# A gated mix of linear attention and a feed-forward block on one core: the attention's middle part cut into smaller steps that one list orders, and its 64-row matmuls padded to 128 rows

## The chip, the core and the metric

The kernel runs on one NeuronCore of one Trainium2 chip. The engines are named as in the profile: PE is TensorE's matmul, PEld its weight load, DVE is VectorE, ACT is ScalarE, POOL is GpSimd, SP is SyncE (here it only issues DMAs). The metric is the device time of one execution in microseconds (us); of several executions the median counts.

## The reference

The input `x` has 2048 tokens of 576 features. Two blocks read it and a sigmoid gate mixes them. All data is float32.

```python
def _A_ref(x, wqkv, wo):                       # 32 heads of 18 features
    q, k, v = qkv[0], qkv[1], qkv[2]
    phi = lambda t: jnp.where(t > 0, t + 1, jnp.exp(t)) + 1e-6
    pq, pk = phi(q), phi(k)
    kv = jnp.einsum("bhsd,bhse->bhde", pk, v)
    z = jnp.einsum("bhsd->bhd", pk)
    num = jnp.einsum("bhqd,bhde->bhqe", pq, kv)
    den = jnp.einsum("bhqd,bhd->bhq", pq, z)[..., None] + 1e-6
    o = num / den
    return (lambda x, *d: x.transpose(*d))(o, 0, 2, 1, 3).reshape(B, S, D) @ wo
...
def _B_ref(x, w_gate, w_up, w_down):           # 4608 hidden features
    h = _gelu(g) * u
    return jnp.einsum("bsf,fd->bsd", h, w_down)
...
g = _sigmoid((x * gate_w).sum(-1, keepdims=True))
return g * a + (1 - g) * b
```

## The kernel before

**Precision.** PE works on a rounded float32 form (`F32R`). So each operand is split into a high part (ACT copies it, which rounds) and a low part (DVE or POOL subtracts the high part from the raw value), and a product is three matmuls: high by high, high by low, low by high. Hence most tiles have two halves.

**Stages.** First come the keys, their sums and the Gram matrices (until about 118 us of the span). Then the attention states are built (to about 146 us). The stage that the change touches comes next, from the masked states to the end of the mixing. Then gate and up projections run as chains of seven products each (a Strassen-like scheme over 2x2 blocks, steps `s1` to `s7`), and last the down projection.

**The stage of the change, step by step.** Tokens go in four blocks of 512 (`b`, in the order 2, 3, 0, 1), features in five groups (`g`), the first four of 128 rows and the last of 64.
- `query(b, g)`: PE multiplies queries into one of three PSUM buffers of the pool `banks` (14 matmuls of 512 columns, 10 in group 4). ACT takes Relu and Exp of it, DVE combines them into `r`. Only then is the buffer free. In group 4 a copy (ACT) and an addition (DVE) come first.
- `wo_load(g)` and `head_out(g)`: the output weight `wo` is loaded and split, PE multiplies it with the states into a buffer of the pool `pair` (two buffers), and ACT and DVE split the result into `KW[g]`. `rows_out` then copies two rows of `KW[4]` into each of the other four by DMA, and `rows_again` repeats the 64 rows of `KW[4]` in its upper half (high part only).
- `halves_of(b, g)` splits `r` into `hl` (two buffers), and `den(b, g)` adds it into the denominators on PE: one or two matmuls of 512 columns.
- `reciprocal(b, h)` inverts the denominators of half a block on DVE and stores them by DMA to DRAM; `reciprocals_load(b, h)` reads them back, spread over the partitions, as `rb`.
- `scale` multiplies `r` by `rb` on DVE, and `scaled_parts` splits the product into `p` (two buffers) on ACT and DVE, for a quarter `t` of a block.
- `mixed(b, t)`: 28 matmuls of 288 columns multiply `p` with `KW` into a `pair` buffer; ACT scales the result by the gate and a DMA stores it. In group 4 the product with the low part of `KW[4]` has only 64 rows (`QR[4]`): two of the 28 matmuls.

Between these stand pieces for later stages: sums of `x` blocks (`ahead_load`, `ahead_sums`, `ahead_store`), sums of up weights (`up_load`, `up_sums`, `up_store`), token sums (`token_load`, `token_sums`), and loads of the first gate and up weights.

**What sets the order.** The kernel is written under a manual schedule: each engine takes its instructions, and each DMA queue its transfers, in the order in which the Python code issues them, and waits at the first one whose operands are not there. In the stage of the change the order is the order of the calls, written out by hand. A pool gives out the buffer whose last reader stands earliest in that order.

Of the kernel before, what the change touches and what calls it, by code (L numbers as in the profile page):

```python
# [30 lines left out]


# [7 lines left out]
def tile_gated_mix(ctx, tc, xt, xs, xn, wk, wv, wq, wo, wgu, wdn, cst, out):  # L40
# [398 lines left out]
    def query(b, g):  # L439
        R = QR[g]  # L440
        if g == 0:
            r_of[b] = (r3p if b == 0 else rp).tile([128, NG, BS], F32, name="r")
            nc.vector.memset(r_of[b][:, NG - 1], 0.0)
        ps = bank()
        r = r_of[b][:R, g]
        ops = []
        for i in range(2):
            x, w = x_slot(b, i), qw[i]
            for kt in range(2):
                hi, lo = Q_HI[kt] + QO[g], Q_LO[kt] + QO[g]  # L450
                ops += [(w[:, hi:hi + 128], x[:, kt]), (w[:, hi:hi + R], x[:, 3 + kt])]
                if g < 4:
                    ops.append((w[:, lo:lo + 128], x[:, kt]))
            ops.append((w[:96, Q_HI[2] + QO[g]:Q_HI[2] + QO[g] + R], x[:96, 2]))
        for k, (wa, xa) in enumerate(ops):
            nc.tensor.matmul(ps[:wa.shape[1]], wa, xa, start=(k == 0), stop=(k == len(ops) - 1), skip_group_check=g == 4)  # L456
        if g == 4:
            nc.scalar.activation(r, ps[64:], AF.Copy)
            nc.vector.tensor_tensor(ps[:R], ps[:R], r, OP.add)
        nc.scalar.activation(r, ps[:R], AF.Relu, scale=-1.0)  # L460
        nc.scalar.activation(r, r, AF.Exp, scale=-1.0)
        nc.vector.scalar_tensor_tensor(r, ps[:R], 0.0, r, op0=OP.max, op1=OP.add)
# [82 lines left out]
    wo_t = {}  # L545

    def wo_load(g):
        raw = w_raw()[:, :D]
        nc.sync.dma_start(raw, wo[g])
# [5 lines left out]
    def states_out():  # L555
# [14 lines left out]
    def key_sums():  # L570
        for g in range(NG):
            R = QR[g]
            sg, z = sel[:R, g * 64:(g + 1) * 64], zc[:R, g:g + 1]
            for rows in (slice(0, R),) if g < 4 else (slice(0, 64), slice(64, 128)):
                nc.vector.tensor_scalar(zmk[rows, g, :64], sg, z, None, op0=OP.mult)
                nc.vector.scalar_tensor_tensor(zmk[rows, g, 64:], sg, z, f32(zmk[:R, g, :64]),
                                               op0=OP.mult, op1=OP.subtract)

    def head_out(g):
        R = VR[g]  # L580
        v = wo_t.pop(g)
        y = pair()
        kh, kl = kvt[:R, 0, g, :R], kvt[:R, 1, g, :R]
        for k, (ka, wl) in enumerate(((kh, 0), (kh, 1), (kl, 0))):
            for n in range(2):
                nc.tensor.matmul(y[:R, n, :288], ka, v[:R, wl, n * 288:(n + 1) * 288],
                                 start=(k == 0), stop=(k == 2))
        w = KW[g].rearrange("p h (n c) -> p h n c", n=2)
        split(w[:R, 0], w[:R, 1], y[:R, :, :288])

    def rows_out():
        for g in range(4):
            nc.sync.dma_start(f32(KW[g][126:]), f32(KW[4][64 + 2 * g:66 + 2 * g]))

    def rows_again():
        nc.scalar.activation(KW[4][64:, 0], f32(KW[4][:64, 0]), AF.Copy)

    hl_of, den_of, rb_of, p_of = {}, {}, {}, {}
    BT = BS // 128

    def halves_of(b, g):
# [8 lines left out]
    def den(b, g):  # L610
# [7 lines left out]

    WO = (4, 0, 1, 2, 3)
    wo_load(WO[0])  # L620
    wo_load(WO[1])
    states_out()
    key_sums()
    query(2, 4)
    halves_of(2, 0)
    halves_of(2, 1)
    query(3, 0)
    for g in range(NG):
        if g + 1 < NG:
            query(3, g + 1)  # L630
        head_out(WO[g])
        if g == 1:
            rows_out()
        if g + 2 < NG:
            wo_load(WO[g + 2])
            if g == 0:
                ahead_store(1)
                ahead_load(3)
                ahead_sums(2)
            elif g == 1:  # L640
                ahead_load(4)
            else:
                ahead_store(2)
                ahead_sums(3)
        elif g + 2 == NG:
            nc.sync.dma_start(xop_d[:, A11], f32(x_slot(2, 0)))
        den(2, g)
        if g + 2 < NG:
            halves_of(2, g + 2)
    ahead_load(5)  # L650
    ahead_sums(4)
    turn.close()
    weights.close()
# [23 lines left out]
    r3p = mixing.pool("r3p")  # L677
    qp = mixing.pool("qp", bufs=2)
    chunks = Scope()
    xcp = chunks.pool("xcp", bufs=2)  # L680

    HB = BS // 2

    def reciprocal(b, h):
        c = slice(h * HB, (h + 1) * HB)
        rb = rb_of[b, h] = qp.tile([128, NG, HB], F32, name="rb", bufs=3)
# [6 lines left out]
    def reciprocals_load(b, h):  # L693
# [6 lines left out]
    def reciprocals(b):  # L700
        for h in range(2):
            reciprocal(b, h)
        for h in range(2):
            reciprocals_load(b, h)

    def scale(b, t):
# [4 lines left out]
    def scaled_parts(b, t):  # L711
        r = r_of[b][:, :, t * 128:(t + 1) * 128]
        p = p_of[b, t] = qp.tile([128, 2, NG, 128], F32R, name="p")
# [4 lines left out]
    def scaled(b, t):  # L718
        scale(b, t)
        scaled_parts(b, t)  # L720

    def mixed(b, t):
        p = p_of.pop((b, t))
        y = pair()
        n = 0
        for g in range(NG):
            for a, wl, R in ((0, 0, 128), (0, 1, QR[g]), (1, 0, 128))[:3 if g < 4 else 2]:
                for i in range(2):
                    nc.tensor.matmul(y[:, i, :288], p[:R, a, g], KW[g][:R, wl, i * 288:(i + 1) * 288],  # L729
                                     start=(n == 0), stop=(n == 13))  # L730
                n += 1
        st = b * BT + t
        o = qp.tile([128, D], F32, name="ga")
# [4 lines left out]
    chunk = {0: Chunk(xcp, 0, 0)}  # L738

    def token_load(kt):  # L740
        chunk[kt] = Chunk(xcp, 0, kt)

    def token_sums(kt, part):
        if part == 0:
            chunk[kt].sums()
        else:
            chunk.pop(kt).summed(nc.gpsimd)

    halves_of(3, 0)
    reciprocals(2)  # L750
    ahead_store(3)
    ahead_store(4)
    ahead_sums(5)
    halves_of(3, 1)
    rows_again()
    nc.sync.dma_start(xop_d[:, A12], f32(x_slot(2, 1)))
    query(0, 0)
    query(0, 1)
    ahead_store(5)
    up_load(0)  # L760
    nc.sync.dma_start(xop_d[:, A22], f32(x_slot(3, 1)))
    den(3, 0)
    halves_of(3, 2)
    den(3, 1)
    halves_of(3, 3)
    query(0, 2)
    up_sums(0)
    up_load(1)
    token_load(1)
    den(3, 2)  # L770
    halves_of(3, 4)
    den(3, 3)
    scaled(2, 0)
    query(0, 3)
    up_sums(1)
    up_load(2)
    den(3, 4)
    scaled(2, 1)
    mixed(2, 0)
    reciprocals(3)  # L780
    query(0, 4)
    up_sums(2)
    up_store(0)
    up_store(1)
    scaled(2, 2)
    token_sums(0, 0)
    mixed(2, 1)
    halves_of(0, 0)
    halves_of(0, 1)
    scaled(2, 3)  # L790
    token_sums(0, 1)
    query(1, 0)
    up_store(2)
    mixed(2, 2)
    den(0, 0)
    halves_of(0, 2)
    query(1, 1)
    scaled(3, 0)
    den(0, 1)
    halves_of(0, 3)  # L800
    mixed(2, 3)
    token_load(2)
    scaled(3, 1)
    token_sums(1, 0)
    query(1, 2)
    den(0, 2)
    halves_of(0, 4)
    den(0, 3)
    mixed(3, 0)
# [438 lines left out]
```

## Time and profile before

| | |
|---|---|
| median of 3 runs | 1516.74 us (1513.53 to 1517.01) |
| the profiled execution | 1514.94 us, span 1513.1 us |
| PE busy | 1500.1 us, 99% of the span |
| DVE, ACT, POOL busy | 1013.6, 549.2 and 717.9 us |
| keys and Gram matrices | to 118 us of the span |
| states | 118 to 146 us |
| the stage of the change | 146 to 293.5 us |
| gate and up chains | 293.5 to about 1112 us |
| down projection | to the end |

The stage of the change ends, on PE, with the last matmul of `mixed(1, 3)`. The first four products of the first gate chain (`first_steps`) stand inside it. A matmul's row in the profile covers its whole way through the array, so rows of successive matmuls overlap: a matmul of 288 columns has a row of some 300 ns, though the next one starts much sooner. How fast PE really goes is read from the distance of starts. Idle time behind a row in square brackets counts only what lies between two such rows.

### The profile page before, as it was taken

How to read it: one execution, taken by the hardware profiler on the slowest of the kernel's cores; microseconds unless marked ns; L12 is line 12 of the kernel's file. 1: busy time of each engine (PE TensorE's matmuls, PEld its weight loads, DVE VectorE, ACT ScalarE, POOL GpSimd, SP SyncE). 2: the span in 40 equal slices, each digit the busy share in tenths (PEclk: the TensorE clock that was granted, in tenths of full speed). 3: DMA queues.
4: the chain of work that ended last, by engine and by line, in shares of the span. 5: the costliest groups of instructions: out<-in, count | busy, mean ns of one | idle time of the engine just before them, and what ended most of it. 6: DMA issues, size and time to landing. Idle time of an engine off the chain costs nothing.

```text
span 1513.1 us, 21566 instructions
## 1 busy us (share of the span) xinstructions
PE 1500.1 (99%) x8312; PEld 1318.2 (87%) x8312; DVE 1013.6 (67%) x1350; ACT 549.2 (36%) x716; POOL 717.9 (47%) x516
## 2 busy tenths in 40 slices
PE   9999999999999999999999999999999999999999
PEld 9999777878888888888888888888899999999999
DVE  8887677485665556665556665556678767777775
ACT  7554545333222332222332222332244344444431
POOL 2663531265645545545545545444257264644620
PEclk9999999999999999999999999999999999999999
DMA  7562473673332223332223322224777656565564
GB/s 248 173 195 87 156 277 141 224 278 109 139 118 91 105 104 139 140 116 93 104 105 139 139 109 101 104 105 166 281 259 276 214 168 214 167 214 179 203 201 134
DMA packets 98751, 246.53 MB, mean 163 GB/s; under 512 B 9104, under 2 KB 36432, under 8 KB 96216
## 3 DMA queue, kind: packets, MB, share of 16 engines
q1 hardware_dynamic: 95768, 235.58, 44.9%
q10 hardware_dynamic: 2880, 9.57, 1.8%
q8 instruction: 65, 1.06, 0.3%
q14 instruction: 38, 0.31, 0.1%
HBM read 156.80 MB, written 88.28 MB: 162 GB/s over the span
## 4 chain that ended last, share of the span: by engine, by line
PE 89%; DVE 3%; DMA 2%; ACT 2%; issue 1%; POOL 1%; SPq 1%; ACTq 0%; DVEq 0%; POOLq 0%
PE bank L878 53%; PE bank L1141 24%; PE pair L729 2%; PE pair L257 2%; PE pair L212 2%; PE kpair L212 2%; PE kpair L257 2%; PE bank L456 1%; DMA xsum_d<-xu 1%; DMA stage<-wdn 0%; DMA xo<-h_d 0%; DVE hl L607 0%; DMA xu<-wgu 0%; POOL wd L1027 0%; DMA raw<-wo 0%
## 5 line engine op out<-in xcount | busy, mean ns | idle before, releaser
L878 PE MATMUL bank<-xo,wg 128*128 128x512 f32 x1764 | 414.4, 395 | 0.6 <-DVE e L910 0.6
L878 PE MATMUL bank<-xo,wu 128*128 128x512 f32 (+1 forms) x1715 | 401.7, 395 | 0.0
L878 PEld LDWEIGHTS bank<-xo,wg 128*128 128x128 f32 x1764 | 332.1, 188 | 79.0 <-DVE e L910 1.0
L878 PEld LDWEIGHTS bank<-xo,wu 128*128 128x128 f32 (+1 forms) x1715 | 323.3, 189 | 75.3
L1149 DVE SCALAR_TENSOR_TENSOR acc<-bank,gate,acc 128x288 f32<-128x288 f32 x288 | 140.0, 512 | 68.7 <-PE bank L1141 65.9
L296 POOL TENSOR_TENSOR stage<-stage 128x384 f32<-128x384 f32 x132 | 153.7, 1184 | 52.2 <-DMA stage<-wgu 49.6
L919 ACT ACTIVATE p<-bank 128x512 f32<-128x512 f32 x72 | 43.0, 597 | 334.4 <-PE bank L878 334.4
L892 POOL TENSOR_TENSOR wg<-stage,wg 128x768 fp32r<-128x768 f32 (+1 forms) x34 | 72.9, 2145 | 178.4 <-ACT wg L891 177.1
L892 POOL TENSOR_TENSOR wu<-stage,wu 128x768 fp32r<-128x768 f32 (+1 forms) x34 | 79.6, 2342 | 147.8 <-ACT wu L891 146.5
L1141 PE MATMUL bank<-wd,xo 128*128 128x288 f32 x1008 | 135.8, 294 | 0.0
L1141 PEld LDWEIGHTS bank<-wd,xo 128*128 128x128 f32 x1008 | 134.1, 188 | 0.0
L1027 POOL TENSOR_TENSOR xo<-stage,xo 128x432 fp32r<-128x432 f32 x44 | 66.3, 1529 | 114.9 <-ACT xo L1025 111.2
L924 DVE TENSOR_TENSOR u<-bank,p 128x512 f32<-128x512 f32 x72 | 49.5, 687 | 94.7 <-PE bank L878 92.3
L1141 PE MATMUL bank<-xo 128*128 128x288 f32 x792 | 107.1, 295 | 0.1
L1141 PEld LDWEIGHTS bank<-xo 128*128 128x128 f32 x792 | 105.7, 188 | 0.5 <-DVE u L913 0.4
L1027 POOL TENSOR_TENSOR wd<-stage,wd 128x432 fp32r<-128x432 f32 x40 | 59.1, 1504 | 89.0 <-ACT wd L1025 89.0
L910 DVE TENSOR_TENSOR e<-bank,u 128x512 f32<-128x512 f32 x54 | 37.2, 691 | 77.3 <-PE bank L878 77.2
L910 DVE TENSOR_TENSOR f<-bank,u 128x512 f32<-128x512 f32 x54 | 37.2, 691 | 72.6 <-PE bank L878 72.3
L900 ACT ACTIVATE f<-f 128x512 f32<-128x512 f32 x54 | 34.1, 632 | 133.5 <-DVE f L910 133.5
L1032 POOL TENSOR_TENSOR stage<-stage 128x432 f32<-128x432 f32 x48 | 75.9, 1607 | 0.0
L938 DVE TENSOR_TENSOR u<-bank,u 128x512 f32<-128x512 f32 x72 | 49.8, 692 | 35.4 <-PE bank L878 33.2
L729 PE MATMUL pair<-kw,p 128*128 128x288 f32 x448 | 67.8, 306 | 1.4 <-ACT p L714 1.4
(197 smaller groups left out, 2324.2 us busy)
## 6 DMA issues: line engine op xcount, KB each, us to landing
h_d<-sx SPq DMA_DIRECT2D x108, 256.0 KB
stage<-wgu SPq DMA_DIRECT2D x34, 768.0 KB
xo<-h_d SPq DMA_DIRECT2D x29, 768.0 KB
e<-h_d SPq DMA_DIRECT2D x28, 768.0 KB
hraw<-h_d SPq DMA_DIRECT2D x27, 768.0 KB
h_d<-e SPq DMA_DIRECT2D x72, 256.0 KB
h_d<-f SPq DMA_DIRECT2D x72, 256.0 KB
stage<-wdn SPq DMA_DIRECT2D x6, 1728.0 KB
```

Source lines behind the costliest of these rows:

```text
L212: nc.tensor.matmul(out_t[:, :n], xa, kvw[i][:rows, r, lo:lo + n], start=(k == 0), stop=(k == 13))
L257: nc.tensor.matmul(y[:, n, :KH], a, p[:, n * KH:(n + 1) * KH], start=(k == 0), stop=(k == len(ops) - 1))
L296: nc.gpsimd.tensor_tensor(o, a, b, OP.subtract)
L729: nc.tensor.matmul(y[:, i, :288], p[:R, a, g], KW[g][:R, wl, i * 288:(i + 1) * 288], start=(n == 0), stop=(n == 13))
L878: nc.tensor.matmul(ps, w_, x_, start=start and i == 0, stop=i == 6, skip_group_check=not start)
L892: nc.gpsimd.tensor_tensor(w[:, i, 3:5], src[:, :, 0:2], f32(w[:, i, 0:2]), OP.subtract)
L910: nc.vector.tensor_tensor(es[i], a, b, OP.add)
L938: nc.vector.tensor_tensor(u3, c, u2, OP.add)
L1027: nc.gpsimd.tensor_tensor(w[:, 1, c], src[:, c], f32(w[:, 0, c]), OP.subtract)
L1032: nc.gpsimd.tensor_tensor(draw[:, o, c], draw[:, x, c], draw[:, y, c], OP.subtract)
L1141: nc.tensor.matmul(y, h[:, hl, g, t * 128:(t + 1) * 128], w[:, wl, g * 288:(g + 1) * 288], start=k in (1, 5) and n == 0, stop=n == len(ops ...
L1149: nc.vector.scalar_tensor_tensor(o, y, gate[:, 1, st:st + 1], o, op0=OP.mult, op1=OP.add)
```

## The change

The steps are cut smaller: `query` into `q` (PE), `qs` (the extra step of group 4), `qe` (ACT) and `qd` (DVE), with `qz` for the memory that has to be zero; `wo_load` into `wl` (load) and `ws` (split); `head_out` into `ho` (PE) and `he` (split); `mixed` into `m` (PE) and `mo` (ACT and store). `scale` and `scaled_parts` become `sc` and `sp`, `halves_of` becomes `h`, `den` becomes `n`, `reciprocal` and `reciprocals_load` become `rc` and `rl`; `ks` is one group of the key sums. One list of words, `PLAN`, says in which order all of them are issued, together with `al`, `as`, `ao`, `ul`, `us`, `uo` (the pieces for later stages), `tl`, `ts`, `tp` (token sums), `ro` and `rd` (the row copies), `xo`, `w`, `g`, `f` (first chain) and `o` (opening and closing of pools). The work itself is the same, with two exceptions: the two 64-row matmuls of `mixed` take all 128 rows, for which the upper half of the low part of `KW[4]` is set to zero once, and `r` is set to zero only where it must be.

```diff
+PLAN = """
+h20 wl4 q24 so q31 al3 h21 ws4 wl0 wl3 qs2 qe24 qz3 ks0 ks2 qe31 wl1 ao1 q30 qd24 ks3 ho4 qd31 ks1 n20 q32 ws0
...
+rl21 q01 qe00 tl0 q02 n30 qe02 qd02 n31 ao3 qd00 h32 qe01 ao5 q03 n32 sc21 ul0 xo2 h33 ul1 sc20 qd01 us0 h34 q04
+qe03 ul2 n33 sp20 n34 rd h00 sp21 rc30 us1 qs0 m20 sc22 m21 rc31 qd03 qe04 sp22 sc23 q11 us2 ts0 q10 tl1 rl30
...
+"""
...
-    def query(b, g):
+    def q(b, g):
...
+    def qe(b, g):
+        ps, r = q_of[b, g][:QR[g]], r_of[b][:QR[g], g]
+        nc.scalar.activation(r, ps, AF.Relu, scale=-1.0)
+        nc.scalar.activation(r, r, AF.Exp, scale=-1.0)
+
+    def qd(b, g):
+        ps, r = q_of.pop((b, g))[:QR[g]], r_of[b][:QR[g], g]
+        nc.vector.scalar_tensor_tensor(r, ps, 0.0, r, op0=OP.max, op1=OP.add)
...
-    def rows_again():
+    def ro(g):
+        nc.sync.dma_start(f32(KW[g][126:]), f32(KW[4][64 + 2 * g:66 + 2 * g]))
+
+    def rd():
         nc.scalar.activation(KW[4][64:, 0], f32(KW[4][:64, 0]), AF.Copy)
+        nc.vector.memset(f32(KW[4][64:, 1]), 0.0)
...
-            for a, wl, R in ((0, 0, 128), (0, 1, QR[g]), (1, 0, 128))[:3 if g < 4 else 2]:
+            for a, wl in ((0, 0), (0, 1), (1, 0))[:3 if g < 4 else 2]:
                 for i in range(2):
-                    nc.tensor.matmul(y[:, i, :288], p[:R, a, g], KW[g][:R, wl, i * 288:(i + 1) * 288],
+                    nc.tensor.matmul(y[:, i, :288], p[:, a, g], KW[g][:, wl, i * 288:(i + 1) * 288],
...
+    for word in PLAN.split():
+        name = word.rstrip("0123456789")
+        steps[name](*map(int, word[len(name):]))
```

The order changes on every engine. Three places show how.

First, the DMA queue of SP from the load of the constants (`cs`) to the copies of two rows into `kw` (`rows_out`). `raw<-wo` are the loads of the output weights, `xu<-xs` and `xsum_d<-xu` loads and stores of the sums for later. Before:

```order
L539 DMA cs<-cst 128x446
L549 DMA raw<-wo 128x576 x3
L315 DMA xsum_d_74<-xu 128x1024
L309 DMA xu<-xs 128x4x256
L593 DMA kw_1883<-kw_1887 2x1152
L593 DMA kw_1884<-kw_1887 2x1152
L593 DMA kw_1885<-kw_1887 2x1152
L593 DMA kw_1886<-kw_1887 2x1152
L549 DMA raw<-wo 128x576
L309 DMA xu<-xs 128x4x256
L549 DMA raw<-wo 128x576
```

The same queue after the change:

```order
L573 DMA cs<-cst 128x446
L583 DMA raw<-wo 128x576
L322 DMA xu<-xs 128x4x256
L583 DMA raw<-wo 128x576 x3
L328 DMA xsum_d_74<-xu 128x1024
L322 DMA xu<-xs 128x4x256
L583 DMA raw<-wo 128x576
L328 DMA xsum_d_75<-xu 128x1024
L631 DMA kw_1884<-kw_1887 2x1152
```

All five loads of `wo` now stand ahead of the row copies; before, two of them stood behind.

Second, DVE around the first two quarters of block 2 that are scaled and split (`r<-r,rb` is `scale`, `p<-r,p` the two subtractions of `scaled_parts`, `r<-bank,r` the last step of a query, `hl<-r,hl` that of `halves_of`). Before:

```order
L709 SCALAR_TENSOR_TENSOR r<-r,rb 128x5x128
L715 TENSOR_TENSOR p<-r,p 128x512
L716 TENSOR_TENSOR p<-r,p 64x128
L462 SCALAR_TENSOR_TENSOR r<-bank,r 128x512
L709 SCALAR_TENSOR_TENSOR r<-r,rb 128x5x128
L715 TENSOR_TENSOR p<-r,p 128x512
L716 TENSOR_TENSOR p<-r,p 64x128
L689 TENSOR_TENSOR rb<-rb,den 40x256
```

After, between the last step of a query and the reciprocals of block 3:

```order
L646 SCALAR_TENSOR_TENSOR hl<-r,hl 128x512
L701 SCALAR_TENSOR_TENSOR r<-r,rb 128x5x128
L646 SCALAR_TENSOR_TENSOR hl<-r,hl 128x512
L701 SCALAR_TENSOR_TENSOR r<-r,rb 128x5x128
L485 SCALAR_TENSOR_TENSOR r<-bank,r 128x512
L646 SCALAR_TENSOR_TENSOR hl<-r,hl 64x512
L707 TENSOR_TENSOR p<-r,p 128x512
L708 TENSOR_TENSOR p<-r,p 64x128
L635 MEMSET kw_1887 64x576
L646 SCALAR_TENSOR_TENSOR hl<-r,hl 128x512
L707 TENSOR_TENSOR p<-r,p 128x512
L708 TENSOR_TENSOR p<-r,p 64x128
```

The scaling and the subtractions of one quarter no longer follow each other on DVE; three other instructions or more stand between them, and the zeroing of `KW[4]` is among them.

Third, PE at the first three queries of block 0 and the denominators of block 3 (the numbers tell the PSUM buffers apart). Before:

```order
L456 MATMUL bank_2194<-xo_116,qw0_121 128x512 x7
L456 MATMUL bank_2194<-xo_116,qw1_122 128x512 x7
L456 MATMUL bank_2212<-xo_116,qw0_121 128x512 x7
L456 MATMUL bank_2212<-xo_116,qw1_122 128x512 x7
L616 MATMUL den_2234<-hl_2164,zmk_1888 128x512 x2
L616 MATMUL den_2234<-hl_2187,zmk_1888 128x512 x2
L456 MATMUL bank_2245<-xo_116,qw0_121 128x512 x7
L456 MATMUL bank_2245<-xo_116,qw1_122 128x512 x7
L616 MATMUL den_2234<-hl_2237,zmk_1888 128x512 x2
```

After:

```order
L467 MATMUL bank_2188<-xo_116,qw0_121 128x512 x7
L467 MATMUL bank_2188<-xo_116,qw1_122 128x512 x7
L467 MATMUL bank_2205<-xo_116,qw0_121 128x512 x7
L467 MATMUL bank_2205<-xo_116,qw1_122 128x512 x7
L467 MATMUL bank_2224<-xo_116,qw0_121 128x512 x7
L467 MATMUL bank_2224<-xo_116,qw1_122 128x512 x7
L655 MATMUL den_2239<-hl_2166,zmk_1888 128x512 x2
L655 MATMUL den_2239<-hl_2173,zmk_1888 128x512 x2
L467 MATMUL bank_2255<-xo_116,qw0_121 128x512 x7
L467 MATMUL bank_2255<-xo_116,qw1_122 128x512 x7
L655 MATMUL den_2239<-hl_2249,zmk_1888 128x512 x2
```

Three queries now stand in a row ahead of the denominators, and only two pairs of denominator matmuls stand between the third query and the fourth, for which one of the three buffers has to be free again.

More of the change, by code (lines that the diff above doesn't have):

```diff
@@ L437, in wv_make @@
         nc.gpsimd.tensor_tensor(w[:, 1], raw, f32(w[:, 0]), OP.subtract)
-    def query(b, g):
+    q_of = {}
+    def q(b, g):
         R = QR[g]
[L441 to L445, printed above, removed]
+        ps = q_of[b, g] = bank()
         ops = []
@@ L617, in den @@
                              stop=g == NG - 1, skip_group_check=True)
[L619 to L653, printed above, removed]
     class Chunk:
@@ L698, in reciprocals_load, with sc @@
                 ap=[[NG * HB, heads], [0, times], [1, NG * HB]]))
[L700 to L706, printed above, removed]
+    def sc(b, t):
         r = r_of[b][:, :, t * 128:(t + 1) * 128]
@@ L759, in tile_gated_mix @@
[L759 to L785, printed above, removed]
@@ L861, in tile_gated_mix, with w_, f_ @@
+    def w_(i):
+        (nc.sync if i else nc.scalar).dma_start(f32(W[i]), wp_d[i])
+    def f_(i):
+        first_steps[i]()
     GATE, UP = 0, 1
```

228 lines of the change are left out of this document (88 added, 140 removed).

## Prediction

> **What bounds the kernel now.** I read the page first, then the windows of the stage that the change touches, then the chain of work and the PE timeline inside it.
>
> ```profile
> PE 1500.1 (99%) x8312; PEld 1318.2 (87%) x8312; DVE 1013.6 (67%) x1350; ACT 549.2 (36%) x716; POOL 717.9 (47%) x516
> PE 89%; DVE 3%; DMA 2%; ACT 2%; issue 1%; POOL 1%; SPq 1%; ACTq 0%; DVEq 0%; POOLq 0%
> ...
> core 0: us, PE busy (x) PEld busy (x) DVE busy (x) ACT busy (x) POOL busy (x), PEclk, DMA share, GB/s
> 145.90:160.00 14.10, 13.04 (x60) 9.98 (x59) 10.62 (x32) 7.72 (x16) 2.81 (x2) 1.00 0.00 1
> 160.00:186.00 26.00, 23.54 (x104) 18.55 (x103) 18.35 (x23) 15.56 (x28) 19.70 (x19) 0.93 0.53 186
> 186.00:205.00 19.00, 18.82 (x102) 15.49 (x101) 11.77 (x16) 7.73 (x14) 2.40 (x4) 1.00 0.87 339
> 205.00:232.00 27.00, 25.65 (x138) 21.02 (x137) 20.77 (x29) 13.70 (x21) 12.68 (x14) 1.00 0.59 203
> 232.00:258.00 26.00, 23.57 (x133) 19.74 (x132) 16.93 (x26) 14.55 (x23) 5.08 (x4) 0.93 0.42 149
> 258.00:293.50 35.50, 35.50 (x226) 31.69 (x225) 18.53 (x26) 13.18 (x18) 7.03 (x4) 1.00 0.64 235
> 321.00:1112.00 791.00, 790.87 (x3413) 641.71 (x3412) 487.07 (x631) 215.62 (x285) 397.80 (x274) 1.00 0.36 130
> ```
>
> PE bounds nearly everything: 89% of the chain, and 790.87 of 791 us in the gate and up chains. What shortens PE's way through the stage of the change (145.9 to 293.5, 147.6 us) therefore shortens the whole, and nothing else there counts. DVE is busy in some 97 of these 147.6 us (the six rows), ACT and POOL less: none of them has too much to do; what they can do is be late.
>
> How much of the 147.6 us is work is read from the chain, where successive matmuls are merged without overlap.
>
> ```profile
> 118.88 3.23 PE bank L456 x14
> ...
> 277.14 16.41 PE pair L729 x112
> ...
> 1146.04 363.74 PE bank L1141 x2745
> ```
>
> A matmul of 512 columns takes 3.23 / 14 = 0.231 us, one of 288 columns 363.74 / 2745 = 0.1325. The stage holds, by the code, 208 wide ones in the queries (twelve of 14, four of 10), 36 in the denominators, 28 in the first gate chain, and 448 of 288 columns in `mixed` and 30 in `head_out`: 272 x 0.231 + 478 x 0.1325 = 62.8 + 63.3 = 126.1 us. So 147.6 - 126.1 = 21.5 us are lost, and they are of three kinds.
>
> *The 64-row matmuls.* The second row of the last fence is four `mixed` without a wait: 16.41 us where 112 x 0.1325 = 14.84 would do, 0.39 us too much in each. The weight loads show where:
>
> ```profile
> 284.81 0.29 PEld L729 LDWEIGHTS pair<-kw,p 64*128 64x128 f32 x2 [0.16 <-issue]
> 285.27 3.49 PEld L729 LDWEIGHTS pair<-kw,p 128*128 128x128 f32 x26 [0.17 <-issue]
> ...
> L729 PE MATMUL pair<-kw,p 64*128 64x288 f32 x32 | 8.4, 344 | 0.0
> ```
>
> The loader stands still for 0.16 us before the two 64-row loads and for 0.17 us after them, waiting for nothing that the profile shows. All 32 of them in 16 `mixed`: 16 x 0.39 = 6.3 us.
>
> *A halved clock.* In two windows the granted clock is 0.93 instead of 1.00. In the PE timeline these are the places:
>
> ```profile
> 169.67 0.63 PE L616 MATMUL den<-hl,zmk 128*128 128x512 f32 x2
> 171.78 0.53 PE L586 MATMUL pair<-wos,kvt 126*126 126x288 f32 x2 [1.48 <-ACT wos L551]
> 173.25 0.79 PE L586 MATMUL pair<-wos,kvt 126*126 126x288 f32 x4 [0.95 <-POOL wos L552]
> ...
> 174.23 8.09 PE L456 MATMUL bank<-xo,qw 128*128 128x512 f32 x28
> ...
> 198.04 4.08 PE L729 MATMUL pair<-kw,p 128*128 128x288 f32 x28
> ...
> 250.03 1.10 PE L616 MATMUL den<-hl,zmk 128*128 128x512 f32 x3 [0.22 <-DVE hl L607]
> 252.13 5.74 PE L729 MATMUL pair<-kw,p 128*128 128x288 f32 x28 [1.01 <-ACT p L714]
> ```
>
> Two queries take 8.09 us, where 2 x 3.23 + 0.16 for the last row's overlap = 6.6 would do, and one `mixed` 5.74 where another takes 4.08: 1.5 + 1.7 = 3.2 us. Both follow a few us in which PE waited again and again.
>
> *Waits.* The rest, 21.5 - 6.3 - 3.2 = 12.0 us: in part the idle times in brackets, in part the slow restart behind each, which rows that overlap hide.
>
> **Part 1: the padding.** It removes 0.39 us from each `mixed`, 6.3 us in all, for every row of 128-row matmuls in a stream goes at 0.1325. It adds one DVE write of 64x576 in `rd`; the nearest row of a DVE instruction of that size is the 0.7 us subtraction in the next fence. Only the last four matmuls of the first `mixed` need it, 24 x 0.1325 = 3.2 us after that starts; so it costs nothing, or at most 0.7 us without that cover. The bounds of the part are 6.3 and 0. A loss is excluded, since the padded loads are of the same shape as the 26 beside them. The rows of the loader decide, and I take 6.3. The Trainium skill speaks against it: "TensorE: Matmul & The Clock Gate", section "LDWEIGHTS (loading the stationary operand)", says that a load's time goes by its columns and that few rows take as long as 128, by which padding would bring nothing and the sum would be 6.3 us smaller; that the loads themselves take as long is so here, but the rows show the loss beside them.
>
> **Part 2: the waits that go.**
>
> ```profile
> 135.44 2.73 SPq L549 DMA_DIRECT2D raw<-wo  x3
> 160.67 2.70 SPq L593 DMA_DIRECT2D kw<-kw  x4
> 164.58 0.61 SPq L549 DMA_DIRECT2D raw<-wo  x1
> 171.04 0.68 ACT L551 ACTIVATE wos<-raw 128x576 fp32r<-128x576 f32 x1 [1.83 <-DMA raw<-wo]
> ...
> L715 DVE TENSOR_TENSOR p<-r,p 128x512 fp32r<-128x512 f32 x16 | 11.3, 705 | 15.3 <-ACT p L714 15.3
> L607 DVE SCALAR_TENSOR_TENSOR hl<-r,hl 128x512 fp32r<-128x512 f32 x16 | 13.5, 870 | 7.7 <-ACT hl L606 7.6
> L709 DVE SCALAR_TENSOR_TENSOR r<-r,rb 128x640 f32<-128x640 f32 x16 | 13.7, 859 | 0.3 <-DMA rb<-rden_d 0.2
> L690 DVE RECIPROCAL rb<-rb 40x256 f32<-40x256 f32 x8 | 14.0, 1745 | 0.3
> L689 DVE TENSOR_TENSOR rb<-rb,den 40x256 f32<-40x256 f32 x8 | 3.1, 388 | 1.7 <-ACT rb L688 1.6
> L301 DVE TENSOR_TENSOR xc<-xc 128x512 f32<-128x512 f32 x3 | 2.2, 739 | 0.1
> L460 ACT ACTIVATE r<-bank 128x512 f32<-128x512 f32 x13 | 7.6, 586 | 7.5 <-PE bank L456 7.5
> L461 ACT ACTIVATE r<-r 128x512 f32<-128x512 f32 x13 | 8.2, 633 | 0.4
> L462 DVE SCALAR_TENSOR_TENSOR r<-bank,r 128x512 f32<-128x512 f32 x13 | 8.7, 676 | 9.4 <-ACT r L461 9.3
> ```
>
> The hole at 170 to 174 is a queue matter: SP cannot issue the row copies before 160.67, since they wait for `KW[4]`, so the last load of `wo` goes out at 164.58, and its split waits until 171.04. In the new order all five loads stand ahead of the copies, where the first three went out at 135.44; the fifth now waits for a store and its buffer, by my walk still some 15 us ahead of its use. This hole and the halved clock behind it go. The others come from DVE: it waits 15.3 us in 16 pieces of nearly 1 us for ACT's half of a split, with denominators' `hl` queued behind. With `sc` apart from `sp` that time is filled with other work.
>
> **Part 3: the waits that come.** I walked the list with these durations. PE's path meets four places:
> - `q03` takes the buffer of `q02`, the first to be free in the list. From the end of `q02`, 0.59 + 0.63 + 0.68 = 1.9 us pass on ACT and DVE, and `qd00`, `h32` are queued behind on DVE; PE has only four denominator matmuls, 0.9 us, meanwhile. With the handoffs 1.2 us.
> - From the end of `n04` DVE owes two reciprocals (2 x 2.13), `h10`, `sc33`, `h11` (0.87, 0.86, 0.87) and 0.7 of `sp32`, 7.6 us, before `m32` can go through; PE has `q14`, `m31`, `n10`, 10 x 0.231 + 3.7 + 0.46 = 6.5. Wait 1.1 us.
> - From `n14` DVE owes `rc10`, two scalings, the token sums of four times 0.74 and `sp02`, 2.13 + 1.72 + 2.96 + 0.7 = 7.5 us; PE has two `mixed` of 3.7. Nothing to 0.5 us, say 0.3.
> - `n01` needs `h01`, which stands on DVE behind the first token sums: some 0.4 us.
>
> Together 3.0 us. That is the lower bound of waiting; the upper is the 12.0 us of before. The walk knows no restart losses and no late DMA, so I take the middle, 7.5 us. No idle of 3 us is left in it, and the 1.06 us in the window from 145.90 left the clock at 1.00; so I count no halved clock.
>
> **The sum.** The stage takes 126.1 + 7.5 = 133.6 us instead of 147.6: 14.0 us less. Behind it everything moves along unchanged if the next weights come in time:
>
> ```profile
> 288.36 0.34 SPq L882 DMA_DIRECT2D stage<-wgu  x1
> 310.02 10.03 PE L878 MATMUL bank<-xo,wg 128*128 128x512 f32 x42
> ```
>
> They are fetched once the last split of `p` frees the memory, 21.7 us before their use. In the new list `m12`'s rest, `m13` and the same ten products follow that split, so the cover stays. The profiled execution of 1514.94 us becomes 1500.9; the median of before lies 1.8 us above it, so I predict 1516.74 - 14.0 = 1502.7 us.
>
> **Rivals.** A measurement of this kernel tells about 0.3%, 4.5 us, from no change.
> - *The new order waits as long as the old, and only the padding counts* (12%): for it speaks that three of the four waits above are DVE queues as before; against it that the 170 hole has one cause, which goes. 6.3 us less, 1510.4.
> - *The padding brings nothing* (4%): the loader stands still at this place whatever the rows, and only the order counts: 14.0 - 6.3 = 7.7 us less, 1509.0. Against it, no other place of the four `mixed` has such a hole. The Trainium skill's rule on loads, above, would have it so.
> - *Almost nothing* (4%): both fall short, within 4.5 us of 1516.74.
> - *Slower, by late reciprocals* (5%). DVE takes its scalings in order, and with `sc21` ahead of `h33`, `qd01` and `h34` a late `rb` now stops the steps that free PSUM buffers and feed the denominators.
>
> ```profile
> 178.65 1.75 DVE L690 RECIPROCAL rb<-rb 40x256 f32<-40x256 f32 x1
> 189.68 0.83 DVE L709 SCALAR_TENSOR_TENSOR r<-r,rb 128x640 f32<-128x640 f32 x1 [0.16 <-DMA rb<-rden_d]
> ```
>
> From the end of the reciprocal (180.4) to its use 9.2 us pass, the last 0.16 of them waiting. In my walk `sc21`, `sc10` and `sc12` come 9 to 10 us behind theirs: at each, what the DMA takes beyond some 10 us is lost one for one. To be slower by 4.5 us it must lose 18.5 us at these three, 6 us each, so 16 us for what took 9.2: 1521. The load of the up weights, issued right behind the last `rb`, speaks for it; the DMA share, 0.64 in the last window of the stage, against it.
>
> **Numbers.** The forecast of waits between 3.0 and about 10 us has 75%. From its lower end, 18.5 us less, 1498.2, and some 1 us for the runs' scatter comes the low end, 1497; the padding alone gives the high end, 1510.5. Faster by over 0.3%: 75 + 12 + 4 = 91%; same 4%; slower 5%.
>
> **What would show it.** Right: the `mixed` without waits at 3.7 us each and no 64-row load among them; no ACT wait for `raw<-wo`; the last matmul of the stage some 14 us before 293.5; PEclk 1.00 throughout; a PE wait ahead of `q03`. The forecast is wrong if the padded `mixed` still takes 4.0 us, if DVE waits for `rb` for microseconds, or if a window shows the halved clock again.

## The result and the profile after

The changed kernel takes 1507.29 us (median of 6 runs, 1506.52 to 1507.93) beside 1515.83 us of the kernel before (6 runs): ratio 0.9945, 95% interval 0.9932 to 0.9957, so 8.5 us less by the medians. Forecast were 14.0 us less, 1502.7 us in a range of 1497 to 1510.5.

The timeline of PE, kernel after (start, us, engine, line, names, shape, count, and in brackets the idle time ahead with what ended it):

```profile
169.88 9.85 PE L467 MATMUL bank<-xo,qw 128*128 128x512 f32 x42
...
181.80 3.55 PE L467 MATMUL bank<-xo,qw 128*128 128x512 f32 x14 [1.14 <-DVE r L485]
...
188.68 7.44 PE L717 MATMUL pair<-kw,p 128*128 128x288 f32 x56
...
203.49 0.50 PE L655 MATMUL den<-hl,zmk 128*128 128x512 f32 x1 [0.22 <-DVE hl L646]
...
229.95 0.50 PE L655 MATMUL den<-hl,zmk 128*128 128x512 f32 x1 [0.25 <-DVE hl L646]
...
231.64 3.46 PE L717 MATMUL pair<-kw,p 128*128 128x288 f32 x24 [0.66 <-DVE p L707]
...
243.90 0.80 PE L655 MATMUL den<-hl,zmk 128*128 128x512 f32 x1 [4.15 <-DVE hl L646]
244.49 13.83 PE L717 MATMUL pair<-kw,p 128*128 128x288 f32 x84
...
273.97 11.64 PE L717 MATMUL pair<-kw,p 128*128 128x288 f32 x84 [1.73 <-ACT p L706]
286.44 5.17 PE L790 MATMUL bank<-xo,wg 128*128 128x512 f32 x21 [0.83 <-ACT ga L724]
...
302.98 7.37 PE L790 MATMUL bank<-xo,wg 128*128 128x512 f32 x31
```

The third chain of products, which began at 310.02, begins at 302.98: 7.0 of the 7.4 us between the two profiled runs (1514.94 and 1507.52) arise ahead of it. The first rows are as forecast: no hole at 170 to 174, a wait at `q03`, two `mixed` without waits in 7.44 us, so 3.7 each, and small waits at `n01` and around `m32`. Three waits were not on the list: 4.15 us ahead of `n14` (the last denominator matmul of block 1), 1.73 ahead of `m11`, 0.83 ahead of the first product behind the stage. And the three `mixed` from 244.49 (`m00` to `m02`) take 13.83 us for 84 matmuls, where 84 x 0.1325 = 11.1 would do. The windows around them show why (columns as in the prediction's windows, the granted clock third from the end):

```profile
238.00:243.30 5.30, 1.75 (x12) 1.31 (x10) 1.87 (x5) 3.94 (x7) 0.00 (x0) 1.00 0.80 278
243.30:250.10 6.80, 6.20 (x25) 6.11 (x26) 6.38 (x9) 1.07 (x3) 0.00 (x0) 0.50 0.66 272
```

The halved clock is there again, for 6.8 us, behind the long idle. So the stage took 286.44 - 146.20 = 140.2 us instead of 147.6. Against the 126.1 us of work that is 14.1 us lost: 2.65 by the clock (13.83 against 11.18 for the same 84 matmuls in the run with a buffer more, below) and 11.5 in waits. Of these 11.5 the brackets above show 8.98 us; the rest, as in the prediction's 12.0, comes out of the difference alone, and no row shows it.

What held `n14` is told by the chain of waits of the kernel after, in the same place (start, us, what):

```profile
229.03 0.75 ACT ga L724
...
229.81 8.48 DMA ga_d<-ga
...
238.37 0.75 ACT ga L724
...
240.09 0.14 ACT L743
240.23 1.15 issue
...
241.50 0.73 ACT p L706
...
243.24 0.61 DVE hl L646
...
243.90 0.80 PE den L655
```

`mo31` writes `ga` at 229.03 and its store goes out at 229.81. `ga` has two buffers, so `mo32` needs the one that this store reads, and the store lands after 8.5 us. ScalarE takes its instructions in the list's order: behind `mo32` (238.37) stand the issue of the gate weights' load (`w0`), the gelu table load (`g`, L743, ending at 241.4), `sp00` (241.50) and only then the first half of `h14`; DVE adds its half, and PE may go on. In the list `mo32` is one entry behind `m32` and eight ahead of `h14`.

### The profile page after: what moved, and what is told of

Read it like the earlier page. It is cut to its first block, busy times and chain, and to the rows that moved or that the text cites. A ratio compares the mean times of both kernels' runs of the same rounds, so it can differ in the third digit from the quotient of the medians.

```text
span 1505.7 us, 21568 instructions
## 1 busy us (share of the span) xinstructions
PE 1490.1 (99%) x8312; PEld 1316.1 (87%) x8312; DVE 1016.9 (68%) x1351; ACT 548.7 (36%) x716; POOL 717.6 (48%) x516
## 4 chain that ended last, share of the span: by engine, by line
PE 96%; DVE 2%; DMA 1%; ACT 1%; issue 0%; SPq 0%; ACTq 0%; DVEq 0%
PE bank L790 54%; PE bank L1050 26%; PE bank L467 4%; PE pair L717 3%; PE pair L270 2%; PE pair L225 2%; PE kpair L270 2%; PE kpair L225 2%; DMA raw<-wk 1%; DMA ga_d<-ga 1%; PE den L655 0%; PE pair L622 0%; PE pair L518 0%; DVE rb L688 0%; ACT ga L724 0%
## 5 line engine op out<-in xcount | busy, mean ns | idle before, releaser
L936 POOL TENSOR_TENSOR wd<-stage,wd 128x432 fp32r<-128x432 f32 x40 | 59.5, 1515 | 89.3 <-ACT wd L934 89.3
L717 PEld LDWEIGHTS pair<-kw,p 128*128 128x128 f32 x448 | 63.1, 196 | 4.1 <-ACT p L706 2.2
```

The lines of the kernel that those rows point to most:

```text
L717: nc.tensor.matmul(y[:, i, :288], p[:, a, g], KW[g][:, wl, i * 288:(i + 1) * 288], start=(n == 0), stop=(n == 13))
L936: nc.gpsimd.tensor_tensor(w[:, 1, c], src[:, c], f32(w[:, 0, c]), OP.subtract)
```

## The experiments

Ratios are to the kernel before, run beside each on the same chip, with the 95% interval behind them; differences to it in us are worked out from the ratio (0.001 is 1.5 us). The medians alone give up to 0.9 us more or less, and the intervals reach 1 to 2.5 us to either side. Edits of the list are shown as the stretch of words that changes, without its line breaks and the words around it; outside the quoted edit a kernel is the one it starts from.

**The padding alone, in the old order.**

```diff
+        nc.vector.memset(f32(KW[4][64:, 1]), 0.0)
...
-            for a, wl, R in ((0, 0, 128), (0, 1, QR[g]), (1, 0, 128))[:3 if g < 4 else 2]:
+            for a, wl, R in ((0, 0, 128), (0, 1, 128), (1, 0, 128))[:3 if g < 4 else 2]:
```

> The kernel before with the padding alone, in the old order. If each mixed loses 0.39 us at its 64-row matmuls whatever its surroundings, the sixteen give 6.3 us: about 1509.5 us beside a before of 1515.8, ratio 0.996, and a mixed without waits takes 3.7 us. If the loader stands still at that place whatever the rows are, nothing: 1515.8, and a mixed still takes 4.0 to 4.1. If the waits on DVE set the pace of the stage, the 0.39 us turn into longer waits ahead of each mixed, and less than half, 3 us, is seen: 1513 or above.

1513.17 us, ratio 0.9991 (0.9982 to 0.9999): 1.4 us less, not 6.3. Its timeline of PE:

```profile
205.26 4.18 PE L730 MATMUL pair<-kw,p 128*128 128x288 f32 x28 [0.77 <-ACT p L715]
...
214.53 3.89 PE L730 MATMUL pair<-kw,p 128*128 128x288 f32 x28
...
310.62 6.94 PE L879 MATMUL bank<-xo,wg 96*128 96x512 f32 x29 [0.50 <-POOL wg L894]
```

The `mixed` is shorter, as the third theory allows too (3.89 us for 4.08 before), but PE then stands 0.77 us ahead of the one at 205.26, where before it stood 0.18, and at 310.62 it waits for weights that were ready before. The rows name ScalarE and POOL there, and DVE at others; most of the 6.3 us turned into waits for them. The profiled run is the shortest of the eleven, and its stage is 3.6 us shorter than before; some 1.4 of these are not the padding, but a halved clock that this run doesn't have (the `mixed` at 251.67 takes 4.17 us, where the one of before takes 5.74).

**The new order alone.**

```diff
-        nc.vector.memset(f32(KW[4][64:, 1]), 0.0)
...
-            for a, wl in ((0, 0), (0, 1), (1, 0))[:3 if g < 4 else 2]:
+            for a, wl, R in ((0, 0, 128), (0, 1, QR[g]), (1, 0, 128))[:3 if g < 4 else 2]:
...
```

> The changed kernel without the padding: the new order alone. If padding and order simply add, the order has brought 8.5 - 6.3 = 2.2 us: about 1513.6 us, ratio 0.9985. If the padding brings nothing and the order is all, 1507.3. The prediction's sum for the order alone was 7.7 us, 1508.1. In the new order the wait ahead of the last denominator of block 1 (4.15 us at 243.90 in the changed kernel) should be shorter or equal if PE arrives there later: it waits for ScalarE and DMA, not for PE.

1509.68 us, ratio 0.9964 (0.9950 to 0.9977): the order alone brings 5.5 us, between the first and third of the numbers expected. The padding adds 0.0019 of 1515, some 2.9 us, here; by the two intervals it can be anything from nothing to 5.7. The wait at `n14`, expected shorter or equal, was longer in its profiled run, the longest of the five (1511.99):

```profile
246.09 0.80 PE L654 MATMUL den<-hl,zmk 128*128 128x512 f32 x1 [4.77 <-DVE hl L645]
```

**The output of `m32` in memory of its own.** The query features of block 3, which nothing reads any more, serve as a third `ga`:

```diff
-        o = pools["q"].tile([128, D], F32, name="ga")
+        if (b, t) == (3, 2):
+            o = r_of[3].rearrange("p g n -> p (g n)")[:, :D]
+        else:
+            o = pools["q"].tile([128, D], F32, name="ga")
```

> The changed kernel, with the output of m32 written into memory of its own (the dead query features of block 3) instead of the ga buffer that the store of m31 still holds. Theory: ScalarE stood 3.02 us at mo32 for that store, with sp00 and h14 queued behind it, and n14 waited for these. Then mo32 runs at about 235.5 instead of 238.4, the gelu table load is over by 238.4, and n14 waits some 1.1 us instead of 4.15: 3.1 us less, and with the long idle goes the halved clock of 243.3 to 250.1, another 2.6 us: 5.7 us less than the changed kernel, about 1501.6 us, ratio 0.991. Rival, late reciprocals: sc00 waits for rb and sets when sp00 can start, so ScalarE only waits at sp00 instead: at most 0.3 us less than 1507.3. Rival, the table load and not the buffer: 1.3 us less at most, 1506.0.

1499.64 us, ratio 0.9897 (0.9884 to 0.9911): 7.6 us less than the changed kernel with its 1507.3. Its timelines of ACT and of PE, and its window to the end of the stage:

```profile
235.70 0.72 ACT L727 ACTIVATE r<-pair,gate 128x576 f32<-128x576 f32 x1
```

```profile
241.10 0.50 PE L655 MATMUL den<-hl,zmk 128*128 128x512 f32 x1 [0.91 <-DVE hl L646]
241.44 11.18 PE L717 MATMUL pair<-kw,p 128*128 128x288 f32 x84
252.46 3.38 PE L793 MATMUL bank<-xo,wg 128*128 128x512 f32 x14
...
266.40 11.34 PE L717 MATMUL pair<-kw,p 128*128 128x288 f32 x84
278.57 5.17 PE L793 MATMUL bank<-xo,wg 128*128 128x512 f32 x21 [0.83 <-ACT ga L727]
```

```profile
238.00:278.60 40.60, 38.86 (x270) 36.81 (x268) 23.91 (x34) 17.10 (x25) 9.06 (x6) 1.00 0.75 265
```

`mo32` runs at 235.70, `n14` waits 0.91 us, and the clock stays at 1.00. The two rivals allowed 0.3 and 1.3 us and fall. (A later run of the changed kernel's very program, below under the up weights, had a median of 1505.78; against that one it is 6.1 us less.) More went than was expected: `m11` (266.40) has no wait either. All from `n14` on came earlier, and the store of `mo02` now goes out at 255.59, 1.1 us ahead of the up weights' load, where in the changed kernel it went out at 261.28, 1.0 behind it. The stage took 278.57 - 146.77 = 131.8 us. The same program, run again later:

> The same program as the run with m32's output in memory of its own, again, on the chip of these runs: the earlier ratio to before was 0.990. If the gain is the buffer's and not that chip's, 0.989 to 0.992 again, without a halved clock in the stage.

1499.73 us, ratio 0.9900 (0.9884 to 0.9917): the gain is the buffer's.

**That kernel without the padding** (the second diff on top of the third).

> The kernel with m32's output in memory of its own, without the padding: what the padding is worth where PE waits little. If the 0.39 us of each mixed is PE's own time and no wait hides it, 6.3 us above that kernel's 1499.6: about 1505.9. If part of the stage still goes at the pace of DVE and ScalarE, as the run of the padding alone in the old order suggests, 2 to 4 us above: 1502 to 1503.5.

1505.89 us, ratio 0.9939 (0.9927 to 0.9951): 6.2 us above 1499.64 to 1499.73. With the largest waits out of the way the padding brings what the rows had promised, and at the matmuls. From the start of `m00` to the start of what follows `m02` PE takes 254.31 - 242.10 = 12.21 us, in the kernel above 252.46 - 241.44 = 11.02: 0.40 us more for each `mixed`, 6.3 for sixteen. Its wait of 1.22 us ahead of `m11`, which the kernel above doesn't have, is made good by waits of 0.34, 0.23 and 0.66 us at 204.12, 230.39 and 232.09 that only that kernel has:

```profile
242.10 12.28 PE L716 MATMUL pair<-kw,p 128*128 128x288 f32 x84
254.31 3.53 PE L792 MATMUL bank<-xo,wg 128*128 128x512 f32 x14
...
270.50 1.67 PE L716 MATMUL pair<-kw,p 128*128 128x288 f32 x9 [1.22 <-ACT p L705]
```

**The old order with the row copies behind the loads of `wo`.**

```diff
-        if g == 1:
-            rows_out()
         if g + 2 < NG:
             wo_load(WO[g + 2])
+            if g == 2:
+                rows_out()
```

> The kernel before with one edit: the four row copies go to the SP queue behind the last load of wo instead of ahead of the last two. Theory: the hole of 170 to 174 is that queue alone. Its two waits of 1.63 and 1.11 us go, and the halved clock of 174.0 to 177.4 with them (1.7 us): 4.4 us less, 1511.4 beside 1515.8, ratio 0.997. Rival: DVE's backlog later in the stage sets the pace, and what PE gains here it waits for at the next denominators: within 1.5 us of before.

1511.43 us, ratio 0.9976 (0.9966 to 0.9986): 3.6 us less, most of the 4.4 expected; the rival, under 1.5, is outside the interval (2.1 to 5.1). From the denominators at 169.67 to those at 182.16 PE took 12.49 us before; here, from 170.16 to 178.13, it takes 7.97. Of these 4.5 us 0.72 came back as a wait for DVE at the next denominator, at 179.71. In its windows PE is busy for all of 170 to 174, and the clock behind is whole:

```profile
170.00:174.00 4.00, 4.00 (x23) 3.43 (x22) 2.67 (x5) 3.07 (x7) 3.77 (x5) 1.00 1.04 357
174.00:180.00 6.00, 5.28 (x23) 4.04 (x22) 5.88 (x8) 4.76 (x9) 5.69 (x6) 1.00 0.35 145
```

If the queue is worth the same in the new order, which was not tried by itself, it is about two thirds of the 5.5 us that the order brings.

**The changed kernel, `h14` and `sp00` ahead of `mo32`.**

```diff
-h13 qd14 m32 mo32 w0 n12 sc00 m33 g sc01 sp00 h14 n13 sp01 n14 mo33 m00
+h13 qd14 m32 n12 h14 sc00 m33 sc01 sp00 mo32 w0 n13 sp01 n14 mo33 g m00
```

> The changed kernel, buffers as they were; in the list only h14 and sp00 go ahead of mo32, and the gelu table load behind mo33. Theory: what holds n14 is ScalarE's order behind a wait for a store, not the buffer as such. ScalarE still waits some 3 us at mo32, but with h14 done; n14 finds its input at 238 to 240, its wait of 4.15 us and the halved clock behind it (2.6 us) go, and at most 1 us comes in ahead of m00, which needs mo32 done: 5.5 to 6.8 us less than the changed kernel, 1500.5 to 1502. Rival: m00 takes over the whole wait, since its PSUM pair is freed by mo32 alone: the same 1507.3, less at most 1 us.

1509.09 us, ratio 0.9954 (0.9941 to 0.9967): nothing gained, but not by the rival. `m00` waits only 0.44 us, and PE now stands at `m02`. Its timelines of ACT and PE:

```profile
242.88 1.28 ACT L743 ACT_TABLE_LOAD   x1 [0.39 <-ACT ga L724]
...
244.41 0.38 ACT L686 ACTIVATE rb<-den 40x256 f32<-40x256 f32 x1
```

```profile
240.24 7.71 PE L717 MATMUL pair<-kw,p 128*128 128x288 f32 x56 [0.44 <-ACT ga L724]
249.25 0.79 PE L717 MATMUL pair<-kw,p 128*128 128x288 f32 x4 [1.30 <-ACT p L706]
251.87 6.12 PE L717 MATMUL pair<-kw,p 128*128 128x288 f32 x24 [1.82 <-DVE p L707]
```

With `h14` out of the way, `n14` went through some 4.5 us earlier, but `mo32`, `mo33` and the table load still stand ahead of `rc10` on ScalarE: its copy of the denominators ran at 244.41, 4.6 us behind `n14` and hardly earlier than the 244.73 of the changed kernel. So DVE's reciprocal, scalings, token sums and `sp02` came no earlier either, and PE waits for them. The last `mixed` of the rows again runs at half the clock (24 matmuls in 6.12 us), and `m11` waits 2.89 us instead of 1.73.

**The up weights later in the list.**

```diff
-sc10 w1 f0 mo02 mo01 f1 m03 sc11 sp10 mo03 sp11 sc12 f2 sc13 m10
+sc10 f0 mo02 mo01 f1 m03 sc11 sp10 mo03 sp11 sc12 f2 sc13 w1 m10
```

> The changed kernel with the load of the up weights (w1, 2240 KB on the SP queue) issued nine entries later in the list, behind sc13. Theory for the second hole (1.73 us ahead of m11): the store of mo02, issued 1 us behind that load, took 9.9 us to land instead of 1.7 to 5, so mo03 and sp11 behind it on ScalarE were late. Then the store lands in under 5 us, and the hole goes: 1.9 us less, 1505.4; the hole at n14 stays at 4.2 us. Rival: the products f0 to f3 or the scalings hold sp11: no change. Risk: the up weights, needed at 291, come late and cost some of it.

The edit changed no engine's order: SP has no other instruction between the old and the new place, and so the theory was not tested. The run tells of the changed kernel's scatter instead: 1505.78 us, ratio 0.9937 (0.9923 to 0.9951), three runs at 1502.7 to 1503.8 and three at 1507.7 to 1507.9. The profiled one is of the lower group; its timelines of PE and ACT:

```profile
241.82 0.50 PE L655 MATMUL den<-hl,zmk 128*128 128x512 f32 x1 [2.57 <-DVE hl L646]
242.16 11.36 PE L717 MATMUL pair<-kw,p 128*128 128x288 f32 x84
```

```profile
267.63 0.74 ACT L724 ACTIVATE ga<-pair,gate 128x576 f32<-128x576 f32 x1 [8.90 <-DMA ga_d<-ga]
```

The same instructions, `n14` waiting 2.57 us instead of 4.15, and no halved clock behind it: 1.6 and 2.5 us, about the 4 us between the groups (the upper group has the lower granted clock, 0.997 to 0.998 against 0.999 to 1.000). And the row of ACT names the store as what `mo03` waited for; in the trace of the kernel after a wait of 7.91 us at the same place is put down to PE.

**The up weights on ScalarE's queue, behind `sp11`.**

```diff
-sc10 w1 f0 mo02 mo01 f1 m03 sc11 sp10 mo03 sp11 sc12
+sc10 f0 mo02 mo01 f1 m03 sc11 sp10 mo03 sp11 w1 sc12
...
-        (nc.sync if i else nc.scalar).dma_start(f32(W[i]), wp_d[i])
+        nc.scalar.dma_start(f32(W[i]), wp_d[i])
```

> The changed kernel with the up weights' load issued by ScalarE's queue behind sp11 instead of by SP, whose queue was free, so that the earlier shift in the list had not moved it by an instruction. Theory: that load, issued 0.3 to 1 us around the store of mo02, is what makes this store take 8 to 10 us, and mo03, sp11 and m11 wait for it. The store then lands in at most 6 us, ScalarE does mo03 some 4 us earlier, PE's wait of 1.7 to 2.1 us ahead of m11 goes, and n14's wait of 2.6 to 4.2 us stays: 2 us less than the changed kernel in the same state of its n14 wait. Rival: the loads of rb, on the same engines, are enough to hold the store: no change.

1503.19 us, ratio 0.9923 (0.9908 to 0.9938). Its timelines of PE and ACT:

```profile
242.66 0.50 PE L655 MATMUL den<-hl,zmk 128*128 128x512 f32 x1 [2.88 <-DVE hl L646]
...
269.65 11.34 PE L717 MATMUL pair<-kw,p 128*128 128x288 f32 x84
```

```profile
264.45 0.74 ACT L724 ACTIVATE ga<-pair,gate 128x576 f32<-128x576 f32 x1 [3.35 <-DMA ga_d<-ga]
```

`mo03` waits 3.35 us for the store of `mo02` instead of 8 to 9, and `m11` no longer waits: the load of 2240 KB was what held it. The time alone does not show that, for the wait at `n14` moved between the runs.

**List alone, the table load behind `sp03`** (the first line of the edit with `g` moved on).

```diff
-h13 qd14 m32 mo32 w0 n12 sc00 m33 g sc01 sp00 h14 n13 sp01 n14 mo33 m00
+h13 qd14 m32 n12 h14 sc00 m33 sc01 sp00 mo32 w0 n13 sp01 n14 mo33 m00
...
-rl11 m02 sp03 o2
+rl11 m02 sp03 g o2
```

> The changed kernel, list alone: h14 and sp00 ahead of mo32, and the gelu table load now behind sp03, where ScalarE has 2.85 us free, instead of behind mo33, where it put rc10 4.6 us behind n14 in the run before. Theory: that run's wait at m02 (1.3 + 1.8 us) came from the table load ahead of rc10; now n14 waits under 1 us, m02 under 1 us, and no halved clock follows: 4 to 6 us less than the changed kernel, 1502 to 1503, with runs closer together. Rival: DVE owes 7.5 us between n14 and sp02 while PE has 7.4, and in the changed kernel the halved clock covered that: m02 still waits 2 us or more, and 1505 to 1507 comes out.

1502.43 us, ratio 0.9917 (0.9902 to 0.9932). The theory's time, but only half its mechanism: in the profiled run, the longest of the four (1504.24), `n14` is free, but `m02` still waits, and its 24 matmuls take 4.97 us where 3.4 would do: the clock is halved for a part of them. `mo32` and `mo33` alone still put `rc10`'s copy 3 us behind `n14`, at 244.95.

```profile
252.39 4.97 PE L717 MATMUL pair<-kw,p 128*128 128x288 f32 x24 [1.80 <-DVE p L707]
```

**All together**, first with the table load behind `mo33` and the up weights' shift in the list that moved nothing, then with both put right. Both also have

```diff
-qe00 tl0 q02 n30 qe02 qd02 n31 ao3 qd00 h32 qe01
+qe00 tl0 qd00 q02 n30 qe02 n31 ao3 h32 qd02 qe01
```

> All together: m32's output in memory of its own, h14 ahead of the scaling and the table load behind mo33, the up weights behind sc13, and qd00 ahead of qd02 so that q03 takes the buffer freed first. Against the kernel with the buffer alone (1499.6) the wait at n14 (1.07 us) and that of q03 (1.3 us) go: 2.0 to 2.4 us less, about 1497.4. Rival: DVE takes both back at the next denominators, since it owes the same work: 1499.6.

1505.13 us, ratio 0.9933 (0.9917 to 0.9949), from 1501.1 to 1509.2: worse than the buffer alone. The profiled run is the shortest of the six and shows a wait at `m02` in its timeline of PE (0.20 and 1.82 us), with the table load ahead of `rc10` again; what the longer ones lost besides, at a granted clock of 0.997, it doesn't show:

```profile
250.31 3.44 PE L717 MATMUL pair<-kw,p 128*128 128x288 f32 x24 [1.82 <-DVE p L707]
```

> All together: m32's output in memory of its own, h14 ahead of the scaling, the table load behind sp03, the up weights on ScalarE's queue behind sp11, qd00 ahead of qd02. Theory: against the kernel with the buffer alone, run beside it here, the waits at q03 (1.3 us) and n14 (1.07 us) go, at most 1 us of it comes back at m02: 1.5 to 2.4 us less. Rival: DVE's backlog gives all of it back: the same.

1499.19 us, ratio 0.9895 (0.9881 to 0.9910), beside 0.9900 of the buffer alone on the same chip. Its timeline of PE:

```profile
238.49 8.44 PE L717 MATMUL pair<-kw,p 128*128 128x288 f32 x60
247.71 3.39 PE L717 MATMUL pair<-kw,p 128*128 128x288 f32 x24 [0.78 <-DVE p L707]
```

The waits at `q03` and `n14` are gone, 0.78 came in at `m02`, and the stage took 277.06 - 145.95 = 131.1 us against 131.8. What remains of the gain is less than these runs can tell from nothing. Either kernel is some 6 to 8 us below the changed kernel and 15 below the one before.

## Why the prediction was right, and where it was not

The sign and the range held; the gain was 8.5 us instead of 14.0. Both parts fell short: the order by itself brought 5.5 us of its 7.7, the padding on top of it some 2.9 of its 6.3.

*The hole at 170 to 174 and its queue*: right, shown in the old order by itself at 3.6 us. By the rows 4.5 us go at that place, the halved clock included, and 0.72 come back.

*The named waits*: right within 0.3 us each. `q03` 1.14 (1.2 forecast), around `m32` 0.66 + 0.25 (1.1), `n01` 0.22 (0.4), `m02` nothing (0.3). Together 2.3 instead of 3.0, by the brackets alone.

*The step that failed* is the sum of part 3, "the walk knows no restart losses and no late DMA, so I take the middle, 7.5 us". The waits measured 11.5, near the upper bound. The walk followed data and PSUM buffers; it did not follow `mo`, whose output buffer is held by a store. The 8.5 us of `mo31`'s store held ScalarE, with `sp00` and `h14` behind it (4.15 us at `n14`); a wait of the same kind at `mo03`, for the store of `mo02`, cost 1.73 at `m11`. With one buffer more the stage lost 131.8 - 126.1 = 5.7 us, less than the 7.5. The 0.83 us behind `m13`, which all traces of the new order shown here have, was not on the list either; its row names ScalarE's last `ga`, but what it hangs on wasn't tried.

*"No idle of 3 us is left in it ... so I count no halved clock"* fell with it: 2.65 us. The prediction's own rows had spoken against it: both of the halved clocks before the change stood behind idles of which the longest row shows 1.48 us.

*DVE's waits for ACT's half of a split*: the theory was that with `sc` apart from `sp` these 15.3 us are filled with other work. In the kernel after the same row (L707) waits 16.5 us, 3.4 of them at the long hole:

```profile
L707 DVE TENSOR_TENSOR p<-r,p 128x512 fp32r<-128x512 f32 x16 | 12.3, 769 | 16.5 <-ACT p L706 16.2
L646 DVE SCALAR_TENSOR_TENSOR hl<-r,hl 128x512 fp32r<-128x512 f32 (+1 forms) x20 | 15.3, 766 | 2.1 <-ACT hl L645 2.0
```

What went is the wait ahead of `hl`, from 7.7 us in 16 pieces to 2.1 in all 20. So the denominators got their input earlier, as forecast, but not by the splits waiting less; which moves in the list did it was not tried one by one.

*Late reciprocals*: of the three signs that were to count against the forecast two appeared, the halved clock above and DVE's waits for `rb`. The groups of the kernel after within the stage, and DVE's timeline:

```profile
L701 DVE SCALAR_TENSOR_TENSOR r<-r,rb 128x640 f32<-128x640 f32 x16 | 13.7, 877 | 2.9 <-DMA rb<-rden_d 2.8
```

```profile
183.32 0.83 DVE L701 SCALAR_TENSOR_TENSOR r<-r,rb 128x640 f32<-128x640 f32 x1 [0.38 <-DMA rb<-rden_d]
...
214.52 1.56 DVE L701 SCALAR_TENSOR_TENSOR r<-r,rb 128x640 f32<-128x640 f32 x2 [1.84 <-DMA rb<-rden_d]
...
237.27 1.56 DVE L701 SCALAR_TENSOR_TENSOR r<-r,rb 128x640 f32<-128x640 f32 x2 [0.61 <-DMA rb<-rden_d]
```

DVE waits 2.8 us for `rb`, where before it was 0.2: 0.38 at `sc21`, 1.84 at `sc30`, 0.61 at `sc00`, and nothing at `sc10` and `sc12`, the other two places named. Behind the first two PE has a single wait of 0.22 us, at 203.49, until 229.95. At `sc00`, ahead of the long hole, it is 0.61 us beside 4.15, and the run with the buffer free got most of that hole back with the `rb` loads as they were. The rival's wait is real, but it is not what the time went to.

*The padding*: 3.7 us each, as forecast. The Trainium skill ("TensorE: Matmul & The Clock Gate", "LDWEIGHTS (loading the stationary operand)") says that a load takes as long with few rows as with 128; that holds for the loads here (0.29 us for two of 64 rows, 0.57 for four of 128), but what would follow, that padding brings nothing, does not: with the buffer free the run without padding is 6.2 us slower. But 6.3 us is PE's own time; what the kernel keeps of it depends on who sets the pace around it: 1.4 us in the old order, some 2.9 in the new (loosely known, see above), 6.2 where the largest holds are gone.

*"Only the padding counts"*: the rows of before and after alone would have led there. 7.4 us less in the stage look like 6.3 of padding, 0.5 of clock and 0.5 of waits. The runs say otherwise: the order alone is 5.5 us, the padding alone 1.4. The two are worth more together (8.3 by the ratio) than one by one, but the difference is within the intervals.

## What to carry to other kernels

A walk of an instruction list must follow the output buffers too: an engine that writes a tile waits for the last store out of it, and everything behind on that engine waits along. Look for late stores ahead of steps that feed the bound engine, and put those steps ahead of the wait, or take a dead tile as a further buffer; but count all that the shift passes: a table load of 1.3 us ahead of the copy that starts the reciprocals went with 2.0 us of waiting at `m02`, and with 0.78 where it stood behind. And a saving counted on the bound engine's own rows is a ceiling: it is kept only where no other engine sets the pace.

## What the runs showed of the hardware

*A store's landing.* 8.5 us passed from the issue of one store of 288 KB to its landing, while the DMA engines were busy for half of the time (the DMA share stands second from the end; kernel after):

```profile
229.80:238.30 8.50, 7.70 (x53) 7.33 (x54) 7.26 (x12) 4.46 (x7) 1.25 (x1) 1.00 0.53 187
```

Two loads of `rb` of 630 KB each went at the same time, issued between 228.4 and 231.5, and a second store of 288 KB from 232.3 on. That these are what slowed the store was argued from this, not tried; for the up weights' load and `mo02`'s store it was tried, above.

*The halved clock.* It followed an idle of 4.15 us for 6.8 us, and one of 2.57 not at all; but it also followed one of 2.88 (84 matmuls in 12.86 us), and two of 1.30 and 1.82 with a few matmuls between them, and before the change two of under 2 us at 170 to 174. The Trainium skill ("TensorE: Matmul & The Clock Gate", "HAM oscillation — how this bites in real kernels") gives as the rule no idle above some 3.4 us. The first two agree; the others show it after less, so a sum that counts no halved clock below 3 us of idle, as the prediction did, is not safe.

The idle times alone do not decide it. Before the change idles of 0.65, 0.22 and 1.01 us stood ahead of the `mixed` at 252.13, which took 5.74 us; with the row copies behind the loads idles of 0.68, 0.23 and 1.01 stood ahead of the same `mixed`, and it took 4.37:

```profile
248.32 4.37 PE L729 MATMUL pair<-kw,p 128*128 128x288 f32 x28 [1.01 <-ACT p L714]
```

Likewise 1.80 us ahead of `m02` in the list alone had it and 0.20 and 1.82 at the same place in the first run of all together did not. What decides was not measured.
